# A recurrence and a highway layer: a new list of all operations, named buffer slots, and matmuls without a weight load

## The chip, the cores and the metric

The kernel runs on one core of one Trainium2 chip. The metric is device time in microseconds (us). Engines: TensorE (PE, its weight loads PEld), VectorE (DVE), ScalarE (ACT), GpSimd (POOL); SyncE (SP) issues nearly all DMAs.

## The reference

Inputs x and f_logit are 4 sequences of 6336 tokens by 256 channels in float32.

```python
sig = 1 / (1 + exp(-f_logit))
f = lower_bound + (1 - lower_bound) * sig
h = 0
for t in range(6336):               # per sequence and channel
    h = f[:, t] * h + (1 - f[:, t]) * x[:, t]
    y[:, t] = h
H = maximum(y @ w_h, 0)             # w_h, w_t: 256 x 256
T = 1 / (1 + exp(-(y @ w_t + b_t)))
out = T * H + (1 - T) * y
```

## The kernel before

The 25,344 tokens are cut into 29 **units** (0 to 28), most of 1024 tokens (128 partitions by 8 blocks); units 0, 1, 27, 28 have 256, units 2 and 26 have 512, and unit 14 takes 192 tokens of each of the four sequences. The 256 channels are two halves of 128 (index 0 and 1). Each unit passes through steps that have one letter each in the code (`do_l` and so on):

- **l**, **x**: load f_logit and x, on SP's queue. **u** (L243, ScalarE): 1 - sigmoid of f_logit.
- **b** (L252): products u·x ("bv"), in quarters of the unit, on GpSimd or, with a "v" behind the token, on VectorE.
- **i** (L259, TensorE): transpose u of one half into PSUM ("uT"). **f** (L274 VectorE, L276 ScalarE): the forget gate from uT.
- **p** (L290, TensorE): transpose the products into PSUM ("bT"). **s** (L307, VectorE): the scan, the recurrence of one half along its tokens; it carries on from the last column of the scan before.
- **z**, **g** (L318, TensorE): y times w_t and y times w_h of one output half, two sums over 128 channels by 512 tokens each. **t** (L331, ScalarE): sigmoid of z. **d** (L336, VectorE): the larger of g (from which y is subtracted by the weights) and -y, scaled.
- **E**, **e** (L342): d·t. E does the first columns in pieces of 512 on GpSimd, e the rest on VectorE; the last number of a unit's line says where the cut lies in its columns (2048 for most units: all on GpSimd; 0: all on VectorE).
- **o** (L361, L362, TensorE): y through a diagonal matrix plus e through an identity, back to tokens. **c** (L372, ScalarE): copy to SBUF. **w** (L379): store, on SP's queue.

The order is written out by hand: `order` is a list of tokens such as `s3.0` (letter, unit, half or part), and each engine's instructions are kept in program order (`pin`), as are SP's DMAs. A number behind a colon names the PSUM slot: two slots "a" of one bank for i and p, three slots "b" of two banks for z, g and o. An instruction that takes a slot waits for the last reader of what lay there. SBUF tiles rotate over `bufs` buffers of a name (l and x 6, u and bv 3, f, y and o 4, t, d and e 2). `shared` (L209) adds one more wait: a GpSimd product (b or E) waits for the last VectorE product (bv or e) ahead of it in the list. Ahead of the units stand the constants: wt and wh load the weights, cc and dg make scale factors and diagonals, WT and WH the scaled weights.

Of the kernel before, what the change touches and what calls it, by code (L numbers as in the profile page):

```python
# [11 lines left out]
FP32 = mybir.dt.float32  # L12
# [7 lines left out]
def kernel(  # L20
# [20 lines left out]
        (0, 128, 2, 0, 'y', 4, 0),  # L41
        (0, 128, 2, 256, 'y', 4, 0),
        (0, 128, 4, 512, 'y', 4, 0),
        (0, 128, 8, 1024, 'y', 4, 1280),
        (0, 128, 8, 2048, 'y', 4, 2048),
        (0, 128, 8, 3072, 'y', 4, 0),
        (0, 128, 8, 4096, 'y', 4, 2048),
        (0, 128, 8, 5120, 'yk', 4, 0),
        (1, 128, 8, 0, 'y', 4, 2048),
        (1, 128, 8, 1024, 'y', 4, 1024),  # L50
        (1, 128, 8, 2048, 'y', 4, 768),
        (1, 128, 8, 3072, 'y', 4, 2048),
        (1, 128, 8, 4096, 'y', 4, 2048),
        (1, 128, 8, 5120, 'y', 4, 768),
        ((0, 1, 2, 3), 128, 6, [6144, 6144, 0, 0], 'yr', 4, 0),
        (2, 128, 8, 192, 'y', 4, 2048),
        (2, 128, 8, 1216, 'y', 4, 768),
        (2, 128, 8, 2240, 'y', 4, 0),
        (2, 128, 8, 3264, 'y', 4, 2048),
        (2, 128, 8, 4288, 'y', 4, 1024),  # L60
        (2, 128, 8, 5312, 'y', 4, 1536),
        (3, 128, 8, 192, 'y', 4, 2048),
        (3, 128, 8, 1216, 'y', 4, 768),
        (3, 128, 8, 2240, 'y', 4, 1024),
        (3, 128, 8, 3264, 'y', 4, 2048),
        (3, 128, 8, 4288, 'y', 4, 2048),
# [4 lines left out]
    bufs = {'l': 6, 'x': 6, 'u': 3, 'bv': 3, 'f': 4, 'y': 4, 't': 2, 'd': 2, 'e': 2, 'o': 4, 'yk': 1, 'yr': 1}  # L71
    order = """
l0 u0 x0 b0.0v i0.0:0 cc f0.0 x1 p0.0:1 p0.1:0 l1 s0.0 u1 l2 dg wh u2 i0.1:1 f0.1v wt i1.1:1 s0.1 i2.0:0 x2
f2.0 WH f1.1 g0.0:0 i1.0:0 b2.0 b1.0v p1.0:1 b2.1 f1.0 l3 x3 WT z0.0:1 t0.0 d0.0 g0.1:2 z0.1:0 p1.1:0 l4 s1.0
s1.1 d0.1 p2.0:1 x4 s2.0 l5 t0.1 u3 g1.0:1 i2.1:0 z1.0:0 i3.0:1 b3.0 f2.1v b3.3v p2.1:0 b3.1 x5 t1.0 f3.0 d1.0
s2.1 z1.1:2 i3.1:1 t1.1 g1.1:0 f3.1 b3.2v p3.0:0 u4 d1.1 e0 b4.0 s3.0 b4.1 z2.0:1 o0.0:2 z2.1:0 t2.0 p3.1:1 l6
g2.1:1 i4.1:0 s3.1 t2.1 b4.3 c0.0 f4.1 x6 l7 g2.0:0 x7 u5 b4.2 b5.0 d2.0 b5.1 d2.1 i4.0:0 e1 f4.0 e2 g3.0:2
z3.0:0 d3.0 p4.0:1 i5.1:0 z3.1:1 t3.0 f5.1 b5.2 b5.3 p4.1:0 o1.0:2 l8 E3.0 g3.1:0 u6 s4.0 b6.0 E3.1 c1.0 t3.1
i5.0:1 s4.1 f5.0 d3.1 o2.0:2 w0.0 b6.2 E3.2 p5.0:0 b6.1 i6.1:1 z4.0:1 g4.0:0 s5.0 d4.0 c2.0 f6.1 t4.0 E4.0
p5.1:1 i6.0:0 z4.1:2 b6.3 u7 e3 o3.1:1 g4.1:0 s5.1 d4.1 t4.1 f6.0 c3.1 o3.0:2 p6.0:1 u8 l10 x8 c3.0 z5.1:1  # L80
p6.1:0 z5.0:0 b7.0 t5.0 s6.0 s6.1 l9 w3.0 i7.0:1 g5.0:2 b7.1 b7.2 x9 g5.1:0 t5.1 f7.0 i7.1:0 b7.3 p7.0:1 d5.0
w3.1 E4.1 E4.2 w2.0 f7.1 u9 g6.0:1 b8.0 i8.0:0 b8.3 E4.3 w1.0 b8.2 d5.1 f8.0 s7.0 z6.0:2 t6.0 b9.0 p7.1:1 l11
i9.0:0 d6.0 g6.1:0 z6.1:2 s7.1 b8.1 u10 f9.0 o4.1:1 b9.1 t6.1 d6.1 i8.1:1 p8.0:0 f8.1 c4.1 e5 x10 z7.0:0
o4.0:2 s8.0 p8.1:1 c4.0 b9.3 b9.2 E6.0 b10.0 o5.0:1 x11 s8.1 z7.1:2 t7.0 c5.0 p9.0:0 g7.0:0 d7.0 t7.1 i9.1:1
u11 o5.1:1 E6.1 s9.0 E6.2 z8.0:2 g7.1:0 f9.1 c5.1 b10.1 i10.1:1 d7.1 f10.1 p9.1:0 E6.3 z8.1:1 g8.0:0 i10.0:1
t8.0 w4.1 s9.1 o6.0:2 t8.1 b11.0 f10.0 d8.0 b10.2 b10.3 o6.1:1 l12 l13 w4.0 E8.0 p10.0:0 c6.0 i11.0:1 x12 w5.0
w5.1 c6.1 b11.2 b11.1 e7 b11.3 s10.0 g8.1:0 f11.0 d8.1 E8.1 o7.1:2 w6.0 x13 u12 i11.1:1 p10.1:0 l14 b12.0 E8.2
w6.1 c7.1 x14 z9.0:1 g9.0:0 t9.0 o7.0:2 s10.1 f11.1 w7.1 p11.0:0 c7.0 w7.0 d9.0 E8.3 z9.1:1 g9.1:0 s11.0
i12.0:1 E9.0 d9.1 b12.2 u13 o8.1:2 l15 p11.1:0 t9.1 b12.1 c8.1 z10.0:1 f12.0 b12.3 t10.0 E9.1 g10.0:0 g10.1:2
s11.1 u14 p12.0:1 i13.1:0 o8.0:1 d10.0 f13.1 c8.0 d10.1 z10.1:0 b13.0 z11.0:2 i12.1:0 g11.0:1 s12.0 E10.0  # L90
t10.1 b13.3 e9 E10.1 f12.1 i13.0:1 b14.0 z11.1:0 b13.2 t11.0 b13.1 e10 x15 p12.1:0 w8.1 o9.0:2 d11.0 l16 s12.1
t11.1 g11.1:1 l17 d11.1 w8.0 b14.1 o9.1:0 f13.0 p13.0:1 i14.1:0 c9.0 c9.1 f14.1 z12.0:2 E11.0 E11.1 g12.0:1
p13.1:0 u15 b14.2 s13.0 t12.0 o10.0:0 b15.0 d12.0 s13.1 i14.0:1 g12.1:1 E11.2 c10.0 d12.1 E11.3 z12.1:2
i15.0:0 f15.0v x16 w9.0 w9.1 o10.1:0 f14.0 p14.0:1 u16 b15.1 b15.2 E12.0 t12.1 g13.0:1 l18 c10.1 s14.0 z13.1:2
i15.1:0 u17 d13.0 f15.1 z13.0:0 p14.1:1 s14.1 E12.1 b15.3 b16.0 o11.1:1 p15.0:0 s15.0 b16.1 t13.0 i16.1:1
g13.1:0 E12.2 c11.1 t13.1 f16.1 o11.0:1 E12.3 g14.0:2 l19 d13.1 d14.0 i16.0:0 u18 p15.1:1 o12.0:0 f16.0
z14.0:2 b16.2 E13.0 c12.0 w10.0 b16.3 x17 i17.0:0 w10.1 s15.1 e13 E13.1 g14.1:0 x18 c11.0 g15.0:1 b17.0 d14.1
b17.2 t14.0 f17.0 p16.0:1 z15.0:2 z14.1:0 b17.1 d15.0 s16.0 b18.0 b17.3 u19 o12.1:1 p16.1:0 t14.1 z15.1:0
w11.1 i18.0:1 w12.0 t15.0 l20 c12.1 b18.1 t15.1 b18.2 o13.0:2 w12.1 g15.1:1 w11.0 o13.1:0 e14 E15.0 x19 E15.1
f18.0 p17.0:1 s16.1 c13.0 b18.3 l21 d15.1 i17.1:0 s17.0 z16.0:2 c13.1 f17.1 g16.0:1 p17.1:0 i18.1:1 o14.0:0  # L100
t16.0 w13.0 x20 o14.1:2 E15.2 u20 c14.1 c14.0 d16.0 s17.1 g16.1:1 w13.1 f18.1 z16.1:2 E16.0 E15.3 p18.0:0 x21
d16.1 t16.1 z17.0:0 E16.1 b19.0 b19.3 p18.1:1 b19.2 g17.0:1 s18.0 b19.1 g17.1:2 t17.0 l22 u21 i19.0:0 f19.0
d17.0 s18.1 w14.1 z17.1:0 t17.1 o15.1:1 e16 i19.1:0 p19.0:1 b20.0 w14.0 x22 b20.1 b20.2 l23 c15.1 f19.1
o15.0:0 d17.1 z18.0:1 g18.0:2 i20.0:0 c15.0 s19.0 b21.0 b20.3 t18.0 g18.1:0 w15.1 f20.0 d18.0 i20.1:1 d18.1
z18.1:1 p19.1:0 f20.1 b21.3 b21.2 p20.0:1 o16.0:2 o16.1:0 t18.1 s19.1 u22 E18.0 e17 c16.0 c16.1 s20.0 E18.1
b21.1 E18.2 b22.0 w15.0 w16.0 E18.3 b22.3 i21.1:0 g19.0:1 z19.0:2 f21.1 t19.0 z19.1:0 t19.1 d19.0 w16.1
i21.0:0 p20.1:1 f21.0 s20.1 g19.1:2 o17.0:1 b22.2 o17.1:0 u23 x23 p21.0:0 c17.1 d19.1 i22.1:1 f22.1 s21.0
o18.0:2 E19.0 c17.0 l27 c18.0 o18.1:0 w17.1 l24 p21.1:1 i22.0:0 z20.0:1 e19 w17.0 s21.1 c18.1 g20.0:2 d20.0
b22.1 t20.0 E19.1 f22.0 b23.0 g20.1:0 x24 l25 w18.0 d20.1 E20.0 i23.1:1 E20.1 b23.3 z20.1:1 p22.0:0 o19.1:2
s22.0 z21.0:0 f23.1 p22.1:1 t20.1 c19.1 t21.0 E20.2 u24 x25 w18.1 b23.2 g21.0:1 o19.0:2 g21.1:0 s22.1 d21.0  # L110
b23.1 E21.0 b24.0 c19.0 i24.0:0 i23.0:1 b24.3 g22.0:2 z21.1:1 b24.1 f24.0 f23.0 p23.0:0 e20 t21.1 d21.1 d22.0
b24.2 p23.1:1 u25 s23.0 E21.1 o20.1:0 z22.0:2 g22.1:1 c20.1 t22.0 i25.1:0 o20.0:0 s23.1 f25.1 c20.0 d22.1
z22.1:2 w19.1 l26 l28 p24.0:1 s24.0 i24.1:0 t22.1 z23.0:1 E21.2 w20.1 E21.3 g23.0:0 o21.1:2 p24.1:1 t23.0
w19.0 d23.0 f24.1 c21.1 E22.0 z23.1:1 i25.0:0 g23.1:0 s24.1 u26 t23.1 x26 f25.0 E22.1 b25.0 o21.0:2 w20.0
g24.0:1 c21.0 b25.3 b25.1 b25.2 p25.0:1 i26.0:0 d23.1 e22 f26.0 E23.0 E23.1 b26.0 e23 d24.0 o22.1:0 b26.1
z24.0:2 c22.1 p25.1:0 z24.1:1 t24.0 t24.1 o22.0:0 o23.1:2 g24.1:1 s25.0 s25.1 c22.0 p26.0:1 d24.1 w21.0 w21.1
s26.0 o23.0:0 c23.1 u27 x28 E24.0 x27 w22.1 c23.0 E24.1 b27.0 g25.0:2 i26.1:0 u28 f26.1 d25.0 E24.2 E24.3
z25.0:1 p26.1:1 z25.1:0 g25.1:2 i27.1:0 t25.0 s26.1 t25.1 o24.0:1 i27.0:1 f27.1 g26.0:0 E25.0 d25.1 c24.0
w22.0 w23.1 f27.0v z26.0:2 p27.0:0 d26.0 s27.0 p27.1:1 z26.1:1 g26.1:0 t26.0 o24.1:2 s27.1 t26.1 c24.1 w23.0
w24.0 d26.1 w24.1 E25.1 E25.2 E25.3 b28.0 i28.0:0 i28.1:1 z27.0:1 o25.0:0 f28.1v t27.0 p28.0:1 g27.0:2 f28.0  # L120
e26 d27.0 s28.0 o25.1:1 p28.1:0 c25.0 c25.1 z27.1:2 o26.0:0 g27.1:1 s28.1 t27.1 c26.0 g28.0:2 d27.1 d28.0
w25.0 z28.0:1 t28.0 g28.1:0 z28.1:2 e27 d28.1 t28.1 e28 o27.0:1 c27.0 w25.1 w26.0 o28.0:0 o28.1:2 w27.0 c28.0
c28.1 w28.0 w28.1
# [6 lines left out]
    st = [dict() for _ in range(NU)]  # L130
    pin = tc.keep_in_program_order

    def sb(shape, dtype, name):
        return pool.tile(shape, dtype, tag=name, name=name, bufs=bufs.get(name, 1))
# [42 lines left out]
    def do_wt():  # L177
        pin(nc.sync.dma_start(w_raw[:, 1], moe_w_t.rearrange("(h p) o -> p h o", p=P)))

    def do_wh():  # L180
        pin(nc.sync.dma_start(w_raw[:, 0], moe_w_h.rearrange("(h p) o -> p h o", p=P)))

    def do_cc():
        prmT = ps.tile([P, 2 * NH], FP32, tag="b0", name="prmT")
        pin(nc.tensor.transpose(prmT, prm, ident_f[:2 * NH, :2 * NH]))
        pin(nc.vector.tensor_scalar(ncc, prmT[:, :NH], 1.0, None, op0=ALU.subtract))
# [47 lines left out]
    def do_l(n, k, eng, slot):  # L234
        load(n, "l", f_logit)

    def do_x(n, k, eng, slot):
        load(n, "x", x)
# [179 lines left out]
```

## Time and profile before

| what | us |
|---|---|
| median of 3 runs (lowest to highest) | 216.46 (216.22 to 217.61) |
| span of the profiled execution | 215.2 |
| the profiled execution's own time | not listed apart from the runs above |
| VectorE busy | 199.2 |
| ScalarE busy | 195.9 |
| TensorE busy (its ends are modelled) | 190.1 |
| GpSimd busy | 178.9 |
| DMA: moved, mean rate | 78.69 MB, 366 GB/s |

The span runs from the first to the last instruction. Busy time is the time in which an engine works on at least one instruction; two instructions of VectorE or ScalarE overlap by some 0.07 us, so that starts tell better than lengths how long one holds the engine. An idle time is put down to what ended it.

### The profile page before, as it was taken

How to read it: one execution, taken by the hardware profiler on the slowest of the kernel's cores; microseconds unless marked ns; L12 is line 12 of the kernel's file. 1: busy time of each engine (PE TensorE's matmuls, PEld its weight loads, DVE VectorE, ACT ScalarE, POOL GpSimd, SP SyncE). 2: the span in 40 equal slices, each digit the busy share in tenths (PEclk: the TensorE clock that was granted, in tenths of full speed). 3: DMA queues.
4: the chain of work that ended last, by engine and by line, in shares of the span. 5: the costliest groups of instructions: out<-in, count | busy, mean ns of one | idle time of the engine just before them, and what ended most of it. 6: DMA issues, size and time to landing. Idle time of an engine off the chain costs nothing. (4 is left out here: it accounts for less than half of the span.)

```text
span 215.2 us, 4648 instructions
## 1 busy us (share of the span) xinstructions
PE 190.1 (88%) x1784; PEld 132.4 (62%) x1811; DVE 199.2 (93%) x164; ACT 195.9 (91%) x195; POOL 178.9 (83%) x166
## 2 busy tenths in 40 slices
PE   7477778988999799999998999999899999999881
PEld 3144456655766666675676766667676576776661
DVE  2789998999999899999998999999999999999960
ACT  4579889999999999999999999999999999999772
POOL 3045789997999999899998999887988999898910
PEclk9999999999999999999999999999999999999999
DMA  6999999999999999999999799998999999498275
GB/s 185 395 420 417 423 419 410 423 316 315 429 416 425 411 426 393 350 411 414 428 425 416 324 329 326 431 399 287 330 412 420 419 422 420 165 321 360 110 285 200
DMA packets 16750, 78.69 MB, mean 366 GB/s; under 512 B 2004, under 2 KB 2776, under 8 KB 11096
## 3 DMA queue, kind: packets, MB, share of 16 engines
q1 hardware_dynamic: 16720, 78.39, 92.7%
q8 instruction: 14, 0.23, 0.4%
q14 instruction: 8, 0.07, 0.1%
q10 hardware_dynamic: 8, 0.00, 0.0%
HBM read 52.43 MB, written 25.95 MB: 364 GB/s over the span
## 5 line engine op out<-in xcount | busy, mean ns | idle before, releaser
L252 POOL TENSOR_TENSOR bv<-u,x 128x512 bf16<-128x512 f16 x95 | 112.8, 1217 | 21.7 <-DVE w_sb L197 9.0
L307 DVE TENSOR_TENSOR_SCAN y<-f,y,bT 128x1024 bf16<-128x1024 f16 (+2 forms) x46 | 92.8, 2032 | 1.6 <-ACT f L276 0.9
L342 POOL TENSOR_TENSOR e<-d,t 128x512 bf16<-128x512 bf16 (+1 forms) x60 | 67.7, 1148 | 3.9 <-DVE e L342 3.0
L336 DVE SCALAR_TENSOR_TENSOR d<-y,ncc,g 128x1024 bf16<-128x1024 bf16 (+2 forms) x54 | 58.9, 1101 | 2.4 <-PE g L318 2.3
L331 ACT ACTIVATE t<-z,bt 128x1024 bf16<-128x1024 f32 (+3 forms) x58 | 57.9, 1019 | 2.0 <-PE z L318 1.3
L276 ACT ACTIVATE f<-uT,ncc 128x1024 f16<-128x1024 f16 (+3 forms) x53 | 55.4, 1057 | 4.2 <-PE uT L259 2.8
L318 PEld LDWEIGHTS <-w_sb 128*128 128x128 f16 x416 | 39.3, 99 | 32.2 <-issue 2.7
L372 ACT COPY o<-op 128x1024 f32<-128x1024 f32 (+2 forms) x53 | 51.2, 983 | 4.7 <-PE op L362 3.1
L243 ACT ACTIVATE u<-l 128x2048 f16<-128x2048 f32 (+3 forms) x29 | 49.2, 1695 | 3.8 <-DMA l<-in_f_logit_dram 3.6
L362 PE MATMUL op<-ident_b,e 128*128 128x128 bf16 x396 | 49.4, 219 | 1.0 <-DVE e L342 0.8
L318 PE MATMUL z<-y,w_sb 128*128 128x512 bf16 (+1 forms) x179 | 47.5, 372 | 1.2 <-DVE d L336 0.2
L318 PE MATMUL g<-y,w_sb 128*128 128x512 bf16 (+1 forms) x181 | 47.9, 372 | 0.7
L362 PEld LDWEIGHTS <-e 128*128 128x128 bf16 x396 | 44.0, 113 | 5.7 <-issue 2.2
L361 PE MATMUL op<-diag,y 128*128 128x128 f16 x368 | 45.9, 219 | 1.6 <-ACT o L372 0.9
L361 PEld LDWEIGHTS <-y 128*128 128x128 bf16 x368 | 41.0, 113 | 1.9
L290 PE MATMUL bT<-ident_f,bv 128*128 128x128 f32 x198 | 33.6, 283 | 7.2 <-POOL bv L252 2.5
L259 PE MATMUL uT<-ident_h,u 128*128 128x128 f16 x396 | 31.9, 221 | 7.7 <-DVE y L307 2.5
L259 PEld LDWEIGHTS <-u 128*128 128x128 f16 x396 | 26.6, 99 | 18.5 <-issue 7.9
L290 PEld LDWEIGHTS bT<-ident_f,bv 128*128 128x128 f32 x198 | 23.1, 142 | 17.0 <-POOL bv L252 3.8
L342 DVE TENSOR_TENSOR e<-d,t 128x512 bf16<-128x512 bf16 (+5 forms) x19 | 17.7, 943 | 1.0 <-PE op L362 0.7
L307 DVE TENSOR_TENSOR_SCAN y<-f,yr,bT 128x1024 bf16<-128x1024 f16 x4 | 9.3, 2333 | 0.0
L252 DVE TENSOR_TENSOR bv<-u,x 128x512 bf16<-128x512 f16 x4 | 3.4, 855 | 3.1 <-DMA x<-in_x_dram 3.1
(42 smaller groups left out, 48.9 us busy)
## 6 DMA issues: line engine op xcount, KB each, us to landing
out_dram<-o SPq DMA_DIRECT2D x46, 512.0 KB, 7.7
l<-in_f_logit_dram SPq DMA_DIRECT2D x22, 1024.0 KB, 11.1
x<-in_x_dram SPq DMA_DIRECT2D x22, 1024.0 KB, 13.8
l<-in_f_logit_dram SPq DMA_DIRECT2D x4, 256.0 KB, 8.7
x<-in_x_dram SPq DMA_DIRECT2D x4, 256.0 KB, 4.5
l<-in_f_logit_dram SPq DMA_DIRECT2D x2, 512.0 KB, 9.7
x<-in_x_dram SPq DMA_DIRECT2D x2, 512.0 KB, 7.5
out_dram<-o SPq DMA_DIRECT2D x3, 256.0 KB, 13.9
```

The source lines that it names most:

```text
L252: shared(pin(e.tensor_mul(st[n]["bv"][:np_, k].rearrange("p d j -> p j d"), st[n]["u"][:np_, q:q + 2], st[n]["x"][:np_, q:q + 2])), not eng)
L259: pin(nc.tensor.transpose(uT[:, j * np_:(j + 1) * np_], st[n]["u"][:np_, j, h * P:(h + 1) * P], ident_h[:np_, :np_]))
L276: pin(nc.scalar.activation(to, of, AF.Identity, scale=ncc[:, h:h + 1], bias=1.0))
L290: pin(nc.tensor.transpose(to, pair, ident_f[:np_, :np_]))
L307: pin(nc.vector.tensor_tensor_scan(y[:, c0:c0 + ln], st[n]["f", h][:, c0:c0 + ln], st[n]["bT", h][:, c0:c0 + ln], 0.0 if prev is None else ...
L318: pin(nc.tensor.matmul(p[:, a:e], w_sb[:, k, ki, m * P:(m + 1) * P], half(n, "y", ki)[:, a:e], start=ki == 0, stop=ki == NH - 1))
L331: pin(nc.scalar.activation(half(n, "t", m), st[n]["z", m][:, :tokens(n)], AF.Sigmoid, bias=bt[:, m:m + 1]))
L336: pin(nc.vector.scalar_tensor_tensor(half(n, "d", m), half(n, "y", m), ncc[:, m:m + 1], st[n]["g", m][:, :tokens(n)], op0=ALU.mult, op1=AL ...
L342: shared(pin(eng.tensor_mul(st[n]["e"][:, a:e], st[n]["d"][:, a:e], st[n]["t"][:, a:e])), eng is nc.gpsimd)
L361: pin(nc.tensor.matmul(o, half(n, "y", h)[:, cols], diag[:, h], start=True, stop=False))
L362: pin(nc.tensor.matmul(o, half(n, "e", h)[:, cols], ident_b, start=False, stop=True))
L372: pin(nc.scalar.copy(o[:np_, :w], st[n]["op", q][:np_, :w]))
```

## The change

The matmuls of z and g: the second of two matmuls with the same weights (the second 512 tokens) is issued as a matmul that loads no weights. Tiles in SBUF get a tag of their own for each slot, and the tokens name the slot where a tile is first made (`l4:4`, `bv` with `b3.1:0`); the number of buffers of each name stays. The transpose of the parameters (`pc`) becomes a token apart from `cc`. The list is new throughout, and so are the cuts between GpSimd and VectorE of 17 units and the choice of the f and b that VectorE does: before f0.1, f2.1, f15.0, f27.0, f28.1 and b0.0, b1.0, b3.3, b3.2; after f0.1, f0.0, f1.1, f1.0, f2.0, f9.0, f17.0, f27.0 and b4.3, b7.0, b19.0.

```diff
     units = [
-        (0, 128, 2, 0, 'y', 4, 0),
-        (0, 128, 2, 256, 'y', 4, 0),
-        (0, 128, 4, 512, 'y', 4, 0),
-        (0, 128, 8, 1024, 'y', 4, 1280),
-        (0, 128, 8, 2048, 'y', 4, 2048),
+        (0, 128, 2, 0, 'y', 4, 256),
+        (0, 128, 2, 256, 'y', 4, 512),
+        (0, 128, 4, 512, 'y', 4, 512),
+        (0, 128, 8, 1024, 'y', 4, 2048),
+        (0, 128, 8, 2048, 'y', 4, 1024),
...
     order = """
-l0 u0 x0 b0.0v i0.0:0 cc f0.0 x1 p0.0:1 p0.1:0 l1 s0.0 u1 l2 dg wh u2 i0.1:1 f0.1v wt i1.1:1 s0.1 i2.0:0 x2
-f2.0 WH f1.1 g0.0:0 i1.0:0 b2.0 b1.0v p1.0:1 b2.1 f1.0 l3 x3 WT z0.0:1 t0.0 d0.0 g0.1:2 z0.1:0 p1.1:0 l4 s1.0
-s1.1 d0.1 p2.0:1 x4 s2.0 l5 t0.1 u3 g1.0:1 i2.1:0 z1.0:0 i3.0:1 b3.0 f2.1v b3.3v p2.1:0 b3.1 x5 t1.0 f3.0 d1.0
-s2.1 z1.1:2 i3.1:1 t1.1 g1.1:0 f3.1 b3.2v p3.0:0 u4 d1.1 e0 b4.0 s3.0 b4.1 z2.0:1 o0.0:2 z2.1:0 t2.0 p3.1:1 l6
-g2.1:1 i4.1:0 s3.1 t2.1 b4.3 c0.0 f4.1 x6 l7 g2.0:0 x7 u5 b4.2 b5.0 d2.0 b5.1 d2.1 i4.0:0 e1 f4.0 e2 g3.0:2
+x0:0 l0:0 wt wh pc:1 l1:1 u0:0 i0.0:1 i0.1:0 u1:1 b0.0:0 cc dg WT f0.1v:0 f0.0v:1 WH p0.0:0 p0.1:1 x1:1 s0.0:0 i1.1:0
+l2:2 s0.1 g0.1:0 b1.0:1 x2:2 i1.0:1 f1.1v:2 u2:2 z0.1:1 f1.0v:3 t0.1:0 i2.0:1 p1.0:0 d0.1:0 z0.0:1 b2.1:2 s1.0:1
+p1.1:0 s1.1 f2.0v:1 l3:3 i2.1:0 x3:3 g0.0:0 g1.1:2 d0.0 g1.0:0 d1.1:1 u3:0 b2.0 d1.0 f2.1:0 i3.0:1 t0.0 b3.1:0 p2.0:0
+f3.0:3 z1.0:2 i3.1:1 b3.2 s2.0:2 e0:0 l4:4 E0.0 p2.1:0 s2.1 t1.0:1 z1.1:0 b3.0 o0.0:1 u4:1 i4.0:0 x4:4 f3.1:2 l5:5
+b3.3 p3.0:1 z2.0:2 t1.1 f4.0:1 b4.3v:1 x5:5 p3.1:0 s3.0:3 c0.0:0 E1.0:1 t2.0:0 b4.0 b4.2 z2.1:1 u5:2 l6:0 g2.1:0 b4.1
+w0.0 d2.1:0 i4.1:1 s3.1 b5.3:2 b5.1 o1.0:2 f4.1:0 l8:1 b5.2 p4.0:1 i5.0:0 x6:0 c1.0:1 t2.1 g3.0:2 u6:0 g2.0:1 z3.0:0
+s4.0:0 p4.1:1 d2.0 t3.0:1 f5.0:3 z3.1:0 w1.0 e2:0 i6.1:0 E2.0 t3.1 b5.0 g3.1:1 s4.1 d3.0:1 u8:1 f6.1:2 E3.1:1 p5.0:1
+b6.1:0 d3.1 g4.1:2 l7:2 b6.3 b6.0 d4.1:0 o2.0:1 x7:1 b6.2 s5.0:1 E3.0 i5.1:0 g4.0:0 c2.0:2 z4.1:2 f5.1:1 p5.1:0 E3.2
...
-e26 d27.0 s28.0 o25.1:1 p28.1:0 c25.0 c25.1 z27.1:2 o26.0:0 g27.1:1 s28.1 t27.1 c26.0 g28.0:2 d27.1 d28.0
-w25.0 z28.0:1 t28.0 g28.1:0 z28.1:2 e27 d28.1 t28.1 e28 o27.0:1 c27.0 w25.1 w26.0 o28.0:0 o28.1:2 w27.0 c28.0
-c28.1 w28.0 w28.1
+g27.1:0 z27.1:2 w24.0 p28.1:1 d27.1:1 c25.0:3 z27.0:0 s28.0:2 w25.1 o26.0:1 s28.1 t27.1:1 w25.0 t27.0 g27.0:2 g28.0:0
+d27.0 z28.0:2 c26.0:2 d28.0:0 g28.1:1 e27:1 d28.1 z28.1:0 t28.0:0 t28.1 o27.0:2 e28:0 c27.0:0 o28.0:1 w26.0 c28.0:1
+w27.0 o28.1:0 c28.1:3 w28.0 w28.1
 """
...
-    def sb(shape, dtype, name):
-        return pool.tile(shape, dtype, tag=name, name=name, bufs=bufs.get(name, 1))
+    def sb(shape, dtype, name, slot=0):
+        return pool.tile(shape, dtype, tag=f"{name}{slot}", name=name)
...
+    def again(out, w, data, start, stop):
+
+        pe = nc.tensor
+        return pe.add_instruction(mybir.InstMatmult(
+            name=nc.get_next_instruction_name(), start_tensor_calc=start, stop_tensor_calc=stop, tile_size=(P, P),
+            tile_position=(0, 0), ldweights=False,
+            ins=[pe.lower_ap(data), pe.lower_ap(w, for_matmul_weights=True)], outs=[pe.lower_ap(out)]))
...
             for a in range(0, N, 512):
                 e = min(a + 512, N)
-                pin(nc.tensor.matmul(p[:, a:e], w_sb[:, k, ki, m * P:(m + 1) * P], half(n, "y", ki)[:, a:e],
-                                     start=ki == 0, stop=ki == NH - 1))
+                if a == 0:
+                    pin(nc.tensor.matmul(p[:, a:e], w, half(n, "y", ki)[:, a:e], start=ki == 0, stop=ki == NH - 1))
+                else:
+                    pin(again(p[:, a:e], w, half(n, "y", ki)[:, a:e], ki == 0, ki == NH - 1))
```

## The prediction

> **What bounds the kernel now.** I read the page first: busy shares, then the span in slices.
>
> ```profile
> PE 190.1 (88%) x1784; PEld 132.4 (62%) x1811; DVE 199.2 (93%) x164; ACT 195.9 (91%) x195; POOL 178.9 (83%) x166
> ...
> DVE  2789998999999899999998999999999999999960
> ACT  4579889999999999999999999999999999999772
> POOL 3045789997999999899998999887988999898910
> ```
>
> VectorE (DVE) is 80% busy or more from the third slice to the thirty-eighth. 215.2 us of span hold 199.2 of its work; the 16 us left lie almost all in the first 15 us and the last 15. ScalarE follows at 195.9. So the end is set by three things: how early VectorE gets into its steady work, how much work its list holds, and what it waits at the end. I read the other engines only where they hold VectorE up.
>
> Second the timeline of VectorE (start, length, line, operation, names, shapes, count, in brackets the idle before):
>
> ```profile
> 18.39 1.24 DVE L252 TENSOR_TENSOR bv<-u,x 128x512 bf16<-128x512 f16 x1
> 19.52 0.46 DVE L336 SCALAR_TENSOR_TENSOR d<-y,ncc,g 128x256 bf16<-128x256 bf16 x1
> 19.91 0.41 DVE L342 TENSOR_TENSOR e<-d,t 128x512 bf16<-128x512 bf16 x1
> 20.24 4.57 DVE L307 TENSOR_TENSOR_SCAN y<-f,y,bT 128x1024 bf16<-128x1024 f16 x2
> ...
> 34.62 2.35 DVE L307 TENSOR_TENSOR_SCAN y<-f,y,bT 128x1024 bf16<-128x1024 f16 x1 [0.71 <-ACT f L276]
> ...
> 56.01 1.22 DVE L342 TENSOR_TENSOR e<-d,t 128x2048 bf16<-128x2048 bf16 x1
> ...
> 70.86 2.29 DVE L342 TENSOR_TENSOR e<-d,t 128x2048 bf16<-128x2048 bf16 x1 [0.71 <-PE op L362]
> ...
> 205.82 0.48 DVE L336 SCALAR_TENSOR_TENSOR d<-y,ncc,g 128x256 bf16<-128x256 bf16 x1 [1.73 <-PE g L318]
> ...
> 210.12 0.43 DVE L342 TENSOR_TENSOR e<-d,t 128x512 bf16<-128x512 bf16 x1 [0.24 <-ACT t L331]
> ```
>
> Three dates matter: 20.24, where the first long scan starts (s3.0: unit 3, half 0); 34.62, where s5.0 starts; 210.55, where the last VectorE operation ends, 4.65 us before the end of the span. Starts show what an operation takes of the engine, 0.07 less than its length: 2.26 a scan of 1024, 1.18 a d of 1024, 0.70 a bv, 0.40 an f of 256.
>
> Third the timelines of GpSimd (POOL) and ScalarE, for what feeds s3.0:
>
> ```profile
> 16.25 2.79 POOL L252 TENSOR_TENSOR bv<-u,x 128x512 bf16<-128x512 f16 x2 [2.70 <-PE uT L259]
> 21.23 4.54 POOL L252 TENSOR_TENSOR bv<-u,x 128x512 bf16<-128x512 f16 x4 [2.19 <-DMA x<-in_x_dram]
> ```
> ```profile
> 19.10 1.90 ACT L243 ACTIVATE u<-l 128x2048 f16<-128x2048 f32 x1
> ```
>
> Unit 3's input x came at 16.15 (a queued load was released then, and GpSimd and VectorE both started its products at 16.2); unit 4's x came at 21.2. Unit 3's products are split, two on GpSimd, two on VectorE (16.18 and 18.39).
>
> Last TensorE in the chain that ended last:
>
> ```profile
> 163.43 0.86 PE z L318 x4
> ```
>
> Four 512-column matmuls with a weight load each take 0.86, 0.215 apiece.
>
> **The weight loads.** Of 416 z and g matmuls 184 come second with the same weights, so 184 loads of 99 ns go: 18.2 us of load time. With 0.1 of load in each step the same four matmuls would need 0.4 of it; op's steps, a load and a matmul each, go by in 0.056, less than the 0.113 of their load row. So loads lie beside matmuls, and I take 0. From above: if a missing load kept the next weights from being loaded early, each of the 92 z and g would show one or two loads, 0.1 to 0.2 us; TensorE's own steps sum to 174 us (85 for z and g, 792 x 0.056 for op, 396 x 0.056 for uT, 198 x 0.11 for bT), so it would stay below VectorE, and only where a g ends VectorE's wait (two such waits in the waits view, 2.3 us) would it be late: at most +3. From below: all of VectorE's waits for TensorE (g 2.3, op 0.7, bT 0.7, z 0.4) gone, -4.1. The page "TensorE: Matmul & The Clock Gate" of the Trainium skill, section "Back-to-back issue gap", gives 131 ns as the sustained spacing for 512 columns and 216 ns for isolated ones; this trace, with 215, stands with the second, loads and all. By the first the 184 matmuls would shrink by 184 x 0.084 = 15 us of TensorE time (an estimate), which could take away at most the 4.1 of waits and give 215.2; nothing in the trace bears it out, and it enters no number here.
>
> **VectorE's list as a whole.** Counted from the two lists. Scans and d: the same. bv: 4 to 3, -0.70. f: one more of 1024 (103.13 shows 1.20) and two more of 256, +2.0. e: 19 in both, but 1280 long 4 to 2, 1536 long 1 to 4, 512 long 5 to 3, 256 long 0 to 1. At 0.73, 0.86 (estimate, on the line from 1280's 0.73 to 2048's 1.13), 0.36 and 0.25 (estimate) that is +0.65. Sum +1.95 us. ScalarE loses three f (-1.9), GpSimd two and a half E and gains a b (-1.9); neither is the bound.
>
> **The start.** Bytes ahead of x3 and x4 are the same in both lists (the weights only move ahead of l1 to x2), so I take 16.15 and 21.2 again. The new list gives all four b3 to GpSimd, with E0.0 (256 long) between: 16.2 + 4.54 + 0.75 = 21.5. It puts b4.3v, which needs x4, on VectorE ahead of s3.0: 21.2 + 0.7 = 21.9. And p3.0 now takes PSUM slot 1 after i3.1, whose reader f3.1 stands behind u4 on ScalarE: 18.7 + 1.9 + 1.1 = 21.7. All three end near 21.7; four transposes (0.5) make s3.0 start at 22.2, not 20.24. VectorE itself would be there by about 19 (s2.0 waits for i3.0, which waits for u3, until 16.4; then s2.0, e0, s2.1), so it idles some 2.5 us at b4.3v. From s3.0: 2.26 + 0.67 + 2.26 gives s4.0 at 27.4; its slot waits for f4.1 behind u5, so 27.6. Then s4.0, d2.0, e2, s4.1, three d: 9.1, and s5.0 starts at 36.7: 2.1 later than 34.62.
>
> What is done by then: against before d4.1 more (+1.18), e shorter (-0.75), three bv fewer (-2.1), three f more (+1.2): 0.45 less. So 1.95 + 0.45 = 2.4 more stands behind s5.0.
>
> Bounds for the 2.1: if the loads landed strictly by bytes issued (the new queue stops at store w0.0, after l6, so less lies behind x4), x3 would come 1.4 earlier and the delay shrink to 0.7; with a further wait of the kind of 34.62 (0.71) it is 2.8.
>
> **The middle.** Before: 0.42 (62.02), 0.71 (70.86), 0.56 (113.55), together 1.7. I keep it. Both ends: 0, and 6 (a wait of 0.3 for each of some 20 units, as the new list has other partners at every wait). The queue of SP: w0.0 now stands ahead of l8 and x6 and waits for c0.0, about 23; l5, x5 and l6 are still in flight then, some 3 MB or 7 us at 420 GB/s, so this costs nothing; were it longer, u6 on ScalarE would be late next. x stands some 1 MB later in the queue at most units, 2.4 us, and GpSimd, having started 7 us earlier relative to its remaining work, covers that.
>
> Port contention: 2048-long e took 1.22, 2.29, 2.05, the 1536 one 1.77 (0.86 expected), one 512 1.09: 3.8 us over the shortest after 34.62. I keep 3.8. Ends: 0, and, as four of five large e paid 0.7 to 1.1 (one 2048 did not), 3.8 + 3 x 0.7 = 5.9 for the three more large ones. The page "SBUF — State Buffer" of the Trainium skill (its list "Reading the diagram") says that a two-input VectorE operation and a GpSimd one exclude each other for a whole instruction. By it the three more large e could pay up to 1.17 each, 3.5, and the sum would be 222.8 (an estimate); the large e of this trace paid 0 to 1.1 over the shortest, which agrees with it but says nothing on how often.
>
> **The tail.** Before, VectorE idled 1.73 + 0.53 + 0.24 = 2.5 at the end, since b28.0, last on GpSimd, ended at 205.1. GpSimd has 162 us of work after b4.1 at 26.6: 188 plus waits (some 10 before, behind its start), so b28.0 is done before VectorE wants it (about 207). What is late next is z28.1 behind c26.0: I keep 0.8. So -1.7. Ends: -2.5 and 0. Behind the last e: 4.65 as before.
>
> **Sum.** 215.2 + 2.1 + 2.4 - 1.7 = 218.0. What lies around the span: the profiled execution's own time isn't listed; the median of the runs, 216.46, is 1.26 above the span, the lowest 1.02. 218.0 + 1.26 = **219.3**.
>
> **The rivals.**
> A, no change (within 1%, 214.3 to 218.6, which is about what a measurement tells from no change): loads land by bytes, so the start costs 0.7, the rest as in the sum: 217.9; or the middle's waits shrink to nothing as well, 216.2. For it: the waits in the middle are small already, and the new list names every slot, so it may have been laid out to fit. Against: three separate paths hold s3.0 at 22.
>
> B, faster: GpSimd's lead. It starts b0.0 at 4.3, not 11.3, and gets ahead of VectorE; if it stays so, its products never lie beside VectorE's e, and the waits that e and GpSimd cause (0.71 at 70.86, 0.56 at 113.55) go too: 219.3 - 3.8 - 1.3 = 214.2. It decides from the point where large e take 1.1 rather than 2. Against: GpSimd has 176 us of work, so it still runs beside most e.
>
> C, slower still: waits of the new order take the place of the old ones in the middle, 3 to 6 us, or the three more large e all meet GpSimd (+2.1, 221.4) and TensorE's missing loads expose the next ones (+3): 221.4 to 225. For it: two engines above 90% in order leave no slack. Against: before has only 1.7.
>
> D, the change does nothing it says: the matmul without a load loads anyway; then the load count stays at 1811 and the time is that of the sum.
>
> **How the numbers follow.** My forecast 0.40 (217.9 to 221), A 0.30, B 0.12, C 0.18; D changes no time and lies within the others. 0.06 of the forecast falls under 218.6, 0.01 of B over 214.3. That gives faster by over 1% 0.11, within 1% 0.30 + 0.06 + 0.01 = 0.37, slower 0.34 + 0.18 = 0.52. The range goes from 215.3 (between A's lower end and B) to 223.5 (middle of C).
>
> **What would show it.** PEld has some 184 fewer instructions and the z row keeps 0.215. s3.0 starts near 22.2 with an idle of about 2 before b4.3v, ended by DMA x; s5.0 near 36.7. VectorE's busy time is near 201, b28.0 ends before 204, the last e ends 4.6 before the end. Wrong I would be if s3.0 starts by 20.5, if the e of 1536 and 2048 all take about 1.1, or if waits for PE or ACT of several us appear between 40 and 200.

## The result, and the profile after

| | us | ratio to before, 95% interval |
|---|---|---|
| before (4 runs beside after) | 217.04 (216.22 to 217.9) | |
| after (4 runs) | **230.05** (229.31 to 230.49) | 1.0583 [1.053, 1.0637] |
| forecast | 219.3 (215.3 to 223.5) | |

Slower, as forecast, but by 13.0 us and not by 2.8. The profiled execution took 229.78, its span is 227.9 (before 215.2).

The page of after, busy shares and slices:

```profile
PE 193.1 (85%) x1811; PEld 132.8 (58%) x1811; DVE 204.0 (90%) x166; ACT 195.5 (86%) x192; POOL 173.4 (76%) x164
...
DVE  1967799999999989998999799599989999999992
ACT  3267989998887899999897999699889999998883
POOL 4355977979399388889659495987898799889930
PEclk9758999999999999999999999999999999999999
```

No engine got much more to do: VectorE's busy time rose most, by 4.8 us, where the forecast had some 2. VectorE's row dips to 7 and 5 in the middle, where before had eights and nines, and the granted clock falls in the first slices. `PEld ... x1811` is the number of before: not one weight load went. The groups by line show them at the line of the new matmuls (count, then busy and mean ns):

```profile
L321 PEld LDWEIGHTS <-w_sb 128*128 128x128 f16 x184 | 17.9, 98 | 20.4 <-issue 6.9
```

VectorE's timeline, the dates that the prediction named and one wait from the middle:

```profile
21.75 0.91 DVE L257 TENSOR_TENSOR bv<-u,x 128x512 bf16<-128x512 f16 x1
24.07 2.35 DVE L313 TENSOR_TENSOR_SCAN y<-f,y,bT 128x1024 bf16<-128x1024 f16 x1 [1.41 <-PE bT L295]
...
38.50 2.34 DVE L313 TENSOR_TENSOR_SCAN y<-f,y,bT 128x1024 bf16<-128x1024 f16 x1
...
146.57 4.58 DVE L313 TENSOR_TENSOR_SCAN y<-f,y,bT 128x1024 bf16<-128x1024 f16 x2 [2.61 <-PE bT L295]
...
223.51 0.42 DVE L356 TENSOR_TENSOR e<-d,t 128x512 bf16<-128x512 bf16 x1 [0.24 <-ACT t L347]
```

s3.0 starts at 24.07 (forecast 22.2), s5.0 at 38.50 (36.7), the last VectorE operation ends 3.97 before the end. Ahead of b4.3 (21.75) VectorE does not wait: the idle of 2 us that the forecast saw there, for the load x4, is missing. The scans at 146.57 are unit 18's. The waits view, before and then after (sum, times, longest):

```profile
POOL bv L252 <- DMA x<-in_x_dram: 7.8, 6, 2.2
...
ACT u L243 <- DMA l<-in_f_logit_dram: 3.6, 5, 1.2
...
DVE y L307 <- PE bT L290: 0.7, 1, 0.7
```
```profile
POOL bv L257 <- DMA x<-in_x_dram: 12.9, 8, 3.2
POOL bv L257 <- DVE e L356: 12.2, 7, 3.9
ACT u L248 <- DMA l<-in_f_logit_dram: 11.7, 11, 2.5
DVE y L313 <- PE bT L295: 9.7, 12, 2.6
```

VectorE's scans now wait for transposed products; those wait for GpSimd's products, and GpSimd and ScalarE wait for loads. SP's own queue says why loads are late. It issues in order, and waits with a store until ScalarE has copied its data (before, then after):

```profile
SPq L379 <- ACT o L372: 103.1, 31, 12.3
```
```profile
SPq L393 <- ACT o L387: 148.3, 39, 13.8
```

SP's waits for a transfer, in the same two views, fell from 40.5 to 5.4 in sum (without the constants and the end). Nor did the loads travel longer (size of each, and median us from issue to landing; before, then after):

```profile
l<-in_f_logit_dram SPq DMA_DIRECT2D x22, 1024.0 KB, 11.1
x<-in_x_dram SPq DMA_DIRECT2D x22, 1024.0 KB, 13.8
```
```profile
l<-in_f_logit_dram SPq DMA_DIRECT2D x22, 1024.0 KB, 8.7
x<-in_x_dram SPq DMA_DIRECT2D x22, 1024.0 KB, 9.9
```

They came late because they went out late: the median load of units 6 to 25 was issued 15.6 us ahead of the start of its first reader in before, 11.3 in after.

One such case in the chain of after, from the copy to the first product of unit 18 (start, length):

```profile
129.64 0.23 ACT o L387
...
129.89 0.34 SPq L393
...
130.33 8.86 DMA x<-in_x_dram
...
139.35 0.23 POOL bv L257
```

The load x18 goes out 0.4 us after store w13.0, which stands a few tokens ahead of it in the list (`w13.0 t15.1:1 s16.0 x18:0`); SP had done nothing else since 121.5. Its buffer was x12's, whose last reader b12.1 ended on GpSimd at 91.3: free for 39 us (in before, 21). The chain leads to the scan at 146.57 and its wait of 2.61.

To compare runs I give each scan a **lateness**: its start, less the VectorE work that stands ahead of it in that run's list (priced by starts as in the prediction). Its growth between two scans is what VectorE lost there.

| lateness, us | s3.0 | s5.0 | s18.0 | s28.0 | growth s5.0 to s18.0 |
|---|---|---|---|---|---|
| before | 6.5 | 7.2 | 10.8 | 14.6 | 3.6 |
| after | 11.4 | 11.5 | 22.5 | 26.3 | 11.0 |
| after without loads of units 6 to 28 | 10.2 | 10.5 | 13.4 | 15.8 | 2.9 |
| before without them | 6.5 | 7.4 | 9.6 | 11.2 | 2.2 |
| after, loads 24 places earlier | 9.9 | 10.2 | 13.6 | 19.4 | 3.4 |
| the same, and E0.0 moved | 10.7 | 12.3 | 15.2 | 19.2 | 2.9 |
| before, loads 13 places later | 5.6 | 5.9 | 24.5 | 32.2 | 18.6 |

The 12.7 us between the spans are: the longer list +1.95, the start +4.3 (to s5.0), the middle 11.0 - 3.6 = +7.4, after s18.0 nothing (3.8 in both), behind s28.0 the rest, -0.95.

### The profile page after: what moved, and what is told of

It reads as the page before. It is cut to its first block, busy times and chain, and to the rows that moved or that the text cites. A ratio compares the mean times of both kernels' runs of the same rounds, so it can differ in the third digit from the quotient of the medians.

```text
span 227.9 us, 4678 instructions
## 1 busy us (share of the span) xinstructions
PE 193.1 (85%) x1811; PEld 132.8 (58%) x1811; DVE 204.0 (90%) x166; ACT 195.5 (86%) x192; POOL 173.4 (76%) x164
## 2 busy tenths in 40 slices
DMA packets 16750, 78.69 MB, mean 345 GB/s; under 512 B 2004, under 2 KB 2776, under 8 KB 11096
## 3 DMA queue, kind: packets, MB, share of 16 engines
q1 hardware_dynamic: 16720, 78.39, 91.6%
## 4 chain that ended last, share of the span: by engine, by line
PE 24%; DMA 13%; DVE 6%; ACT 6%; POOL 5%; issue 5%; SPq 3%; ACTq 0%; DVEq 0%; POOLq 0%
DMA out_dram<-o 5%; PE op L377 4%; PE op L376 4%; DMA x<-in_x_dram 4%; DMA l<-in_f_logit_dram 4%; PE z L334 3%; PE bT L295 3%; PE g L334 3%; POOL e L356 3%; SPq L393 3%; DVE y L313 3%; DVE d L351 3%; PE g L321 2%; PE z L321 2%; PE uT L264 2%
## 5 line engine op out<-in xcount | busy, mean ns | idle before, releaser
L257 POOL TENSOR_TENSOR bv<-u,x 128x512 bf16<-128x512 f16 x96 | 111.1, 1183 | 34.6 <-DMA x<-in_x_dram 12.9
L356 POOL TENSOR_TENSOR e<-d,t 128x512 bf16<-128x512 bf16 (+1 forms) x57 | 63.1, 1124 | 10.1 <-DVE e L356 4.3
L347 ACT ACTIVATE t<-z,bt 128x1024 bf16<-128x1024 f32 (+3 forms) x58 | 56.8, 996 | 8.8 <-PE z L321 3.6
L281 ACT ACTIVATE f<-uT,ncc 128x1024 f16<-128x1024 f16 (+3 forms) x50 | 52.0, 1050 | 3.2 <-PE uT L264 2.2
L387 ACT COPY o<-op 128x1024 f32<-128x1024 f32 (+2 forms) x53 | 50.1, 964 | 4.4 <-PE op L377 3.0
L295 PE MATMUL bT<-ident_f,bv 128*128 128x128 f32 x198 | 32.9, 281 | 10.2 <-POOL bv L257 3.5
L334 PE MATMUL z<-y,w_sb 128*128 128x512 bf16 (+1 forms) x108 | 38.0, 371 | 3.5 <-ACT o L387 1.5
L334 PE MATMUL g<-y,w_sb 128*128 128x512 bf16 (+1 forms) x108 | 38.0, 373 | 1.7 <-ACT t L347 0.9
L295 PEld LDWEIGHTS bT<-ident_f,bv 128*128 128x128 f32 x198 | 22.5, 142 | 18.6 <-POOL bv L257 5.8
L334 PEld LDWEIGHTS <-w_sb 128*128 128x128 f16 x232 | 23.2, 101 | 17.0 <-issue 1.7
L321 PE MATMUL g<-y,w_sb 128*128 128x512 bf16 x84 | 31.9, 379 | 0.0
L321 PE MATMUL z<-y,w_sb 128*128 128x512 bf16 x84 | 31.8, 379 | 0.0
L321 PEld LDWEIGHTS <-w_sb 128*128 128x128 f16 x184 | 17.9, 98 | 20.4 <-issue 6.9
```

Source lines behind the costliest of these rows:

```text
L257: shared(pin(e.tensor_mul(st[n]["bv"][:np_, k].rearrange("p d j -> p j d"), st[n]["u"][:np_, q:q + 2], st[n]["x"][:np_, q:q + 2])), not eng)
L281: pin(nc.scalar.activation(to, of, AF.Identity, scale=ncc[:, h:h + 1], bias=1.0))
L295: pin(nc.tensor.transpose(to, pair, ident_f[:np_, :np_]))
L321: return pe.add_instruction(mybir.InstMatmult(name=nc.get_next_instruction_name(), start_tensor_calc=start, stop_tensor_calc=stop, tile_si ...
L334: pin(nc.tensor.matmul(p[:, a:e], w, half(n, "y", ki)[:, a:e], start=ki == 0, stop=ki == NH - 1))
L347: pin(nc.scalar.activation(half(n, "t", m), st[n]["z", m][:, :tokens(n)], AF.Sigmoid, bias=bt[:, m:m + 1]))
```

## The experiments

**Theory S**: the loads of the new list stand too near their readers and behind stores, on a queue that stops at each store. **Rivals**: P, GpSimd's added wait for VectorE's e (`shared`); T, traffic, loads and stores in each other's way; W, the new matmul; and the start.

### The parts of the change

The old list with named slots and the new matmul (the diff's `again` and tags, none of its list):

> The old list of operations with the rest of the change: every SBUF tile in a named slot (the slot whose last reader stands earliest in the list), the second of two matmuls issued without a weight load. If the list alone is what costs (L), the time is that of before, 216 to 218, with 1811 weight loads or 184 fewer. If the matmul without a load costs anything (M), it is 219 to 229.

216.94, ratio 1.0041 [1.0005, 1.0076]. So the list, with its cuts between GpSimd and VectorE, costs the 13 us. The weight loads number 1811 here as well.

The list with ordinary matmuls:

```diff
-                if a == 0:
+                if True:
```

> The changed kernel with ordinary matmuls, each with its weight load. The trace of the changed kernel still shows 1811 loads, so (L) expects no change: 229 to 231. (M) expects 3 to 12 us less.

229.33, 1.0598 [1.0523, 1.0672]: W falls; the new form of matmul neither gains nor costs.

### GpSimd's wait

```diff
-        elif held:
+        elif False:
```

> The changed kernel without the added wait of a GpSimd product for the VectorE product ahead of it in the list. Theory P: this wait (16.5 us of GpSimd idle time ended by a VectorE e, against 5.2 before) makes products, their transposes and the scans late: 222 to 226, with the scans' 9.7 us of waits for bT down to some 3, and GpSimd's waits for a VectorE e gone. Theory S (loads stand behind stores): within 2 us of 230. Large e on VectorE may get longer in both.

230.69, 1.0659 [1.0567, 1.0751]. GpSimd only waits for something else, in the view of its waits:

```profile
POOL bv L257 <- DMA x<-in_x_dram: 20.2, 9, 4.1
```

12.9 became 20.2: the load was behind the wait for e all along. P falls.

### The loads

Each load as early as its buffer's last reader allows:

```diff
-b17.2 z15.1:2 f17.0v:2 u18:2 w13.0 t15.1:1 s16.0 x18:0 E14.0
+b12.0 s11.1:2 b12.1 x18:0 t9.0 f12.1:0 o8.0:1
```

> The changed kernel with SP's queue alone reordered: each load moved up to where the last reader of its buffer stands in the list, loads and stores each in their old order. Theory S: loads come late because they stand behind stores that wait for ScalarE (148 us of SP waits, 103 before; GpSimd waited 12.9 us for x, ScalarE 11.7 for l): 222 to 226, those waits down to 8 and 4. Theory P: within 2 us of 230, the waits for DMA become waits for VectorE's e.

244.06, 1.1286 [1.1197, 1.1375]: a miss. Now a load that waits for its buffer holds up the stores behind it, and ScalarE's copies wait for those:

```profile
ACT o L384 <- DMA out_dram<-o: 19.1, 6, 5.8
```

So "as early as can be" isn't the cure; the queue blocks both ways. Next, no loads at all (units 6 to 28 compute on the inputs of units 3 to 5, so this part of the input is left out), in the new list and in the old:

```diff
     def load(n, name, src, slot):
+        if n >= 6:
+            st[n][name] = st[3 + n % 3][name]
+            return
```

> The changed kernel without the loads of units 6 to 28: they compute on the inputs of units 3 to 5, which stay in their buffers (part of the computation is left out, the output is that of other data). Theory S (late loads): the list loses nothing by its order of the engines, so it ends 4 to 6 us above the old list treated the same way (2 of VectorE work, 3 of start). Theory O (the order of the engines makes the waits): the distance stays 10 to 13.

> The kernel before with the same left out, the measure for the run above. Both theories: 209 to 215, since VectorE's 199 us of work stay and the wait for the last x (195.6) goes.

220.2 (1.0111 [1.005, 1.0172]) and 214.04 (0.9855 [0.9775, 0.9935]). Of the 13 us 6.2 are left: the list 1.95, the start 3.1 (10.5 - 7.4 in the table; it was 4.3 in after) and about 1 behind it. The middle grows by 2.9 and 2.2. The middle of after is lost to loads. The same with the loads kept, moved by at most 24 places of the list:

```diff
-g2.1:0 b4.1 w0.0 d2.1:0 i4.1:1 s3.1 b5.3:2 b5.1 o1.0:2 f4.1:0 l8:1 b5.2 p4.0:1 i5.0:0 x6:0
+f3.1:2 b3.3 l8:1 p3.0:1 z2.0:2 t1.1 x6:0 f4.0:1 b4.3v:1
```

> The changed kernel with each load moved up by at most 24 operations of the list (some 6 us), never past the last reader of its buffer. Theory S: loads earlier without stores held up, 224 to 227. Theory O: 229 to 231.

223.29, 1.0199 [1.0078, 1.032]; some 7 us less than after; the middle grows by 3.4 as in before (behind s18.0 5.8 are still lost, in after 3.8). GpSimd's and ScalarE's waits for loads fell from 24.6 to 12.9:

```profile
ACT u L245 <- DMA l<-in_f_logit_dram: 8.8, 5, 2.8
...
POOL bv L254 <- DMA x<-in_x_dram: 4.1, 2, 2.6
```

What is left lies in the first 35 us. Past 35 us the two waited 12.7 us for loads in after, 3.8 in before and not at all here; the scans waited 6.0, 0 and 2.2 us for transposed products.

The other way round, the old list with loads later. Counted over units 6 to 25, the median distance from a load to its first reader is 39.5 places in the old list, 27.5 in the new, 54.5 in the run above, 25.5 in this one.

```diff
-E13.1 g14.1:0 x18 c11.0 g15.0:1 b17.0 d14.1 b17.2
+E13.1 g14.1:0 c11.0 g15.0:1 b17.0 x18 d14.1 b17.2
```

> The kernel before with each load from unit 6 on moved up to 13 places later in the list, no nearer than 11 places to its first reader, so that the median distance from a load to its first reader is 25.5 places (39.5 in the list of before, 27.5 in that of after, 54.5 in the run that moved the new list's loads ahead). Nothing else changes. Theory S (late loads cost the middle of the new list) expects the loss of that middle here too: 221 to 225 us, with waits of GpSimd's bv for x and of ScalarE's u for l of some 20 us or more (11.4 before). If it is the new order of the compute operations and not the distance of the loads, 216 to 218.5.

234.96, 1.0801 [1.0713, 1.0889]: the place of the loads alone makes the fast list slower than after. The mechanism is as expected, the size 10 us above the expected range. The loss comes in a few long stops (the longest of SP at a store 21.0 us, in before 12.3); its waits for loads:

```profile
POOL bv L251 <- DMA x<-in_x_dram: 23.0, 9, 6.3
ACT u L242 <- DMA l<-in_f_logit_dram: 18.1, 9, 9.3
```

And the old list with loads up to 24 places earlier (`e13 E13.1 g14.1:0 x18` becomes `E12.2 c11.1 x18 t13.1`):

> The kernel before with each load moved up by at most 24 operations of its list. Without loads it gained 3 us, so late loads cost it that at most: 214 to 216 if the move helps here too; 217 to 221 if stores then hold up ScalarE's copies.

222.41, 1.0258 [1.0191, 1.0324]. Copies wait 11.4 us for stores here: the old list stood near its best distance, with a loss on both sides. The earlier loads of the new list without `shared`'s wait:

> The new list with loads 24 operations earlier and without the added wait of GpSimd for VectorE's products. With the loads in time GpSimd still waits 22 us for VectorE's e: theory P, second form, expects 220 to 222; if GpSimd has slack in this list, 223 to 224.

231.8 (228.38 to 242.04), too scattered for an interval; no sign of a gain: its lowest time is 4 us above the highest with `shared`'s wait, 223.96.

### Stores on a queue of their own

If SP's order is all, ScalarE may issue the stores:

```diff
-            pin(nc.sync.dma_start(dst, src))
+            pin(nc.scalar.dma_start(dst, src))
```

> The kernel after with one edit: the stores w are issued by ScalarE, at the same places of the list, and SP's queue holds loads alone. Theory S (the middle is lost because loads stand on SP's queue behind stores that wait for ScalarE's copies) expects 220 to 224 us, the size that moving loads 24 places ahead gave (223.3) or that having no loads gave (220.2), less than 4 us of wait of GpSimd's bv and ScalarE's u for loads (24.6 before the edit), and ScalarE longer by about 59 issues. Rival T (the new order as such, or DMA rate lost by mixing loads with stores) expects 228 to 232, with those waits as they were.

> The kernel before with the same edit: stores issued by ScalarE. Theory S expects little to gain, since before loses only 3.6 to 7.8 us of waits for loads off the path: 215 to 218 us. If the issue of 59 stores costs ScalarE some 0.1 us each and ScalarE is near the path, 219 to 222; then the first run's gain is understated by as much.

> The kernel with the new list and each load as early as its buffer allows (244.06 us when stores shared SP's queue), now with the stores issued by ScalarE. Theory S says that the 244 came from stores standing behind loads that waited for their buffers: with queues apart neither waits for the other, 219 to 224 us, and ScalarE's waits for a store's end fall from 19 us to under 4. Rival T (traffic: early loads and stores share the DMA engines and stores come late for that) expects 235 or more.

245.0 (1.1343 [1.1292, 1.1395]), 245.94 (1.1373 [1.1318, 1.1428]) and 244.12 (1.1305 [1.1255, 1.1355]): all three miss, and the third lies where T was expected. Up to s16.0 S holds: between s5.0 and s16.0 the first loses 3.5 where after loses 7.7, and the third 3.5 where the same list with all on SP's queue loses 18.7. Then ScalarE itself stops at the stores (in the first, five issues over 8.17 us), and what waits for ScalarE stops too:

```profile
159.47 1.10 ACT L281 ACTIVATE f<-uT,ncc 128x1024 f16<-128x1024 f16 x1
159.90 8.17 ACTq L393 DMA_DIRECT2D out_dram<-o  x5
168.18 1.11 ACT L281 ACTIVATE f<-uT,ncc 128x1024 f16<-128x1024 f16 x1 [7.61 <-DMA out_dram<-o]
```

The old list loses as much in all. How much of this stop is traffic these runs do not say, and why an issue on ScalarE waited for an earlier transfer is open. The Trainium skill's page "DMA: Bandwidth & Descriptors", section "Issuing engines are not separate DMA queues", says that transfers from several issuing engines run interleaved on the same 16 engines and that only issue time is saved; no run here was faster in all for a second issuer.

### The start

New list up to s5.0, the old one behind it:

> The new list up to s5.0, the old list for all that is left (slots given anew). The lateness of VectorE's scans against its work in the list is 11.5 us at s5.0 in the new list and 7.2 in the old one. If the start costs what it shows and the rest is as before: 216.5 + 4.3 + 0.5 of work = 221. If the old list's slack takes the late start in: 217 to 219.

230.42, 1.0582 [1.052, 1.0643]: inconclusive. The seam made a stall of its own, SP at a store from 30 to 52 us, lateness 12.9 at s5.1 and 19.6 at s6.0; by itself another case of S. Then the loads 24 places earlier, with VectorE taking b3.2 and b3.3, GpSimd b4.3, and f3.1 moved ahead of u4:

> The new list with loads 24 operations earlier (223.3) and its start changed at the three places that hold s3.0: b3.2 and b3.3 on VectorE, b4.3 on GpSimd, f3.1 ahead of u4. If the three paths of the prediction are what makes the start late, s3.0's lateness falls from 9.9 us to 7 to 8 and the time to 220.5 to 222. If the start is late for another reason (loads, clock), 223 to 224.

224.51, 1.0325 [1.0242, 1.0408]: a miss, s3.0 at 25.18, since u4 slid to 21.23 and i4.0, ahead of p3.0 on TensorE, waited for it. Then twelve idle matmuls between 5 and 10 us:

```diff
+    def do_kk(slot):
+        for _ in range(6):
+            pin(nc.tensor.matmul(idle[:, :512], zeros[:, :P], zeros, start=True, stop=True))
```

> The changed kernel with twelve more matmuls on zeros between 5 and 10 us, where TensorE is busy 1.1 us of 5 and the granted clock then falls to 0.50 until 20. If the clock costs at the start, s3.0's lateness falls from 11.4 to 10.2 us (as in two runs whose clock stayed at 1.00) and the time by about 1 us, to 229. If not, within 0.4 of 230, or above for the added work.

230.39, 1.059 [1.0518, 1.0662]. TensorE's matmuls are faster in this start: two z matmuls of 256 columns take 0.38 at 11.82, in after 0.63 at 11.45. s3.0's lateness goes from 11.4 to 10.9, the time stays: the slow matmuls of the start cost half a us at s3.0, and nothing in the end. Last, GpSimd's E0.0, which waited 2.31 for VectorE's e0 in after, with b3.0 and b3.3 behind it:

```profile
20.27 0.67 POOL L356 TENSOR_TENSOR e<-d,t 128x256 bf16<-128x256 bf16 x1 [2.31 <-DVE e L356]
20.90 2.74 POOL L257 TENSOR_TENSOR bv<-u,x 128x512 bf16<-128x512 f16 x2
```
```diff
-b3.2 s2.0:2 e0:0 l4:4 E0.0 p2.1:0 s2.1 t1.0:1 z1.1:0 b3.0 o0.0:1 u4:1 i4.0:0 x4:4 f3.1:2 l5:5 b3.3 p3.0:1
+b3.2 s2.0:2 e0:0 l4:4 p2.1:0 s2.1 t1.0:1 z1.1:0 b3.0 u4:1 i4.0:0 x4:4 f3.1:2 l5:5 b3.3 E0.0 p3.0:1
```

(o0.0 goes behind p3.1.)

> The kernel after with E0.0 (GpSimd) moved behind b3.3, and o0.0, which reads it, behind p3.1. If GpSimd's wait of 2.31 us for VectorE's e0 ahead of E0.0 sets the first long scan, b3.3 ends near 21 and s3.0 starts near 23.2, where f3.1 and the transposes of p3.0 behind it end, instead of 24.07. Whether the 0.9 us stays to the end is open: theory S, by which loads set the pace from unit 5 on, expects 229 to 230; if the start's delay is carried through, 229.1 or less. If another path sets it, s3.0 stays at 24.

228.99 (227.37 to 231.19), 1.0579 [1.0481, 1.0677]; s3.0 at 22.22, yet s5.0 at 38.00: most of the gain is gone by then, 1.23 us in a wait for g at 25.79. Of the 1.85 gained at s3.0 some 1.2 are not the move's: here no early VectorE operation met a product of GpSimd, as one did in after (last section). Both moves together:

> The new list with its loads at most 24 places earlier (223.29 us alone) and E0.0 moved behind b3.3 with o0.0 behind p3.1 (228.99 alone). If the first long scan is then set by GpSimd's products, it starts near 21.7; if by b4.3 on VectorE, which waits for x4, near 22.3 as in the two parts. 221.5 to 223.5 in all; under 221 would say that the start weighs more than its date tells.

223.61, 1.0307 [1.0235, 1.0379]: no better than the loads alone. s3.0 came at 23.42 here, where one did. No version that computes the whole beat before.

## Why the prediction was wrong in size

In spans, the forecast was 2.8 and 12.7 came; the 9.9 between are 1.8 from the start, 7.4 from the middle and 0.75 from the tail. What lies around the span adds 0.9: it was taken as 1.26, a median less another execution's span, and is 1.7 to 2.0 wherever time and span of one execution are both on record; the rest is that after's profiled execution lies 0.3 below the median.

- **The middle** is the step that failed: "I keep it", and with it "x stands some 1 MB later in the queue at most units, 2.4 us, and GpSimd ... covers that". I priced the bytes ahead of a load and not the time at which SP may issue it. One MB later in the queue meant, counted in the two lists, two more stores ahead of a load (median over units 6 to 28; three at x18), each with a wait for a copy that could last 13.8 us. Measured: 7.4 us, where the term's own upper end, 6, was taken for other waits. Taking the loads away and moving them 24 places both bring the growth back to 2.9 to 3.4, and moving the old list's loads makes it there: the cause is shown. The price per place is not: 13 places cost 18.6 - 3.6 = 15 us in the old list. "So this costs nothing", said of w0.0 alone, held: SP stood there until 24.4, and no load was waited for between 16 and 65 us. The last of the signs of being wrong came: scans waited 6.0 us for TensorE's products past 35 us.
- **The start.** s3.0, forecast at 22.2, came at 22.61 and 22.22 in two runs with the new list, and at 24.07 in after. That it came near is in part luck. The forecast had s2.0 start at 16.4 and VectorE idle before b4.3; s2.0 started at 17.5 to 18.7 in these three runs, VectorE reached b4.3 at 21.0 to 21.8 without a wait for x4. Between 22.61 and 24.07 lie two things not foreseen. VectorE's second operation of the WH step met a product of GpSimd (last section), and all up to e0 came 1.07 later (19.86 against 18.79); and b3.0 with b3.3, beside b4.3 on VectorE, took 2.74 instead of 2.29. s5.0, forecast at 36.7, came at 37.2 and 38.0 in those two runs; which path holds the scans between isn't settled.
- **VectorE's list**: +1.95 stands; the 6.2 us left between the two runs without loads have room for it, the start's 3.1 and little more.
- **Port contention**: e took 18.0 in sum before and 18.4 after (+0.65 by length forecast). The three more large e did not all pay: the four of 1536 took 0.95, 1.93, 1.38 and 1.19, against 0.86 expected alone, and the three of 2048, which had taken up to 2.29, 1.20 to 1.23.
- **The weight loads** cost nothing, but not for my reason: they were not left out. That was rival D.
- **The tail** gained 0.95 instead of 1.7: b28.0 ended at 218.7, 1.1 before s28.0, not before 204. GpSimd has no lead at the end of this list, and the loads are not why: without them b28.0 ended at 208.2, 1.1 before s28.0 too.

Rival C had the right kind (new waits in the middle) and named the wrong ones. Slower transfers (T) are not what made the loads late in after, since they landed sooner after issue than in before. Open are the start's last path, how much traffic adds to each late load's trip (8.86 us for x18), and ScalarE's stop in the runs with stores apart.

## What to carry to other kernels

On an in-order DMA queue count, for each load, not the bytes ahead of it but the stores ahead of it that wait for a compute engine, and how long before its reader the load can really go out. Price an order by the time at which its buffer was free against the time of issue: 39 us lay between them for x18, 21 in before. Then check both ways: loads pulled too far ahead wait for their buffers and hold the stores.

## What the runs showed of the hardware

- A matmul issued with its weight load off still had one: 184 loads at its line, and 0.215 us from one 512-column matmul to the next, as before.
- Whether a short VectorE operation meets a GpSimd product differs between runs of the same instructions. In after one did, and took 1.26 where its twin took 0.27 (VectorE, then GpSimd):

```profile
8.13 1.26 DVE L210 TENSOR_SCALAR w_sb<-w_raw,cc 128x128 f16<-128x128 f32 x1
...
9.57 0.27 DVE L210 TENSOR_SCALAR w_sb<-w_raw,cc 128x128 f16<-128x128 f32 x1
```
```profile
8.11 1.20 POOL L257 TENSOR_TENSOR bv<-u,x 128x512 bf16<-128x512 f16 x1 [2.07 <-DMA x<-in_x_dram]
```

  It ended at 9.39, 0.08 after the product. With ordinary matmuls the twin took 1.25, and in the two runs with s3.0 at 22.2 and 22.6, and in the one without loads, both took 0.27. The Trainium skill's page "SBUF — State Buffer", list "Reading the diagram", says that when GpSimd meets a VectorE operation of certain kinds, those with two inputs in SBUF among them, whichever starts first holds the shared ports for its whole instruction. The dates agree; that this operation is of such a kind no run here shows.
- The granted clock of the profile did not tell how fast TensorE ran at the start. Two z matmuls of 256 columns took 0.63 to 0.64 in after (11.45, granted clock 0.50) and in the two runs with s3.0 at 22.2 and 22.6 (10.25 and 10.37, granted clock 1.00). In before, at 1.00 throughout, they took 0.64 at 11.53 and 0.38 at 14.40. Nor did it follow TensorE's busy time: 1.83 of the 5 us from 5 to 10 were followed by 0.50 in before without loads, 1.34 by 1.00 in the last run with stores apart.
- The same 78.69 MB held SP's DMA queue for 91.6% of 16 engines' 227.9 us, 208.8, against 92.7% of 215.2, 199.5, before.
